# Another order of the first batch's loads, with a new job order and new PSUM banks, in a fused Linformer attention and MLP mixer

## The chip, the cores and the metric

The kernel runs on one core of one Trainium2 chip. The metric is the time of one execution in microseconds (us) on the device. The kernel before took 418.57 us, the median of 3 runs (417.91 to 418.78). One further execution was profiled. All instruction times below come from that one.

## The reference

```python
# q, k, v: (8 batches, 8 heads, 1024, 64); E, F: (64, 1024)
k_proj = einsum('ks,bhsd->bhkd', E, k)
v_proj = einsum('ks,bhsd->bhkd', F, v)
scores = scale * matmul(q, k_proj^T)              # 1024 x 64 for each head
attn = softmax(scores)
x = matmul(attn, v_proj)                          # -> (8, 1024, 512), heads side by side
h = maximum(x^T @ w_tok1, 0) @ w_tok2             # tokens: 1024 -> 256 -> 1024
u = x + h^T
h2 = maximum(u @ w_ch1, 0) @ w_ch2                # channels: 512 -> 1536 -> 512
out = u + h2                                      # (8, 1024, 512) float32
```

## The kernel before

The work is a pipeline over eight batches. The kernel does not emit its instructions as it goes through its loops. It first collects some 2,200 jobs in a `Planner` (each job is a few instructions of one engine, or one DMA) together with what each job reads and writes. `plan()` then returns the jobs in one sequence, and the last loop (L1521) emits them in that sequence, so each engine and each DMA queue gets its own jobs in the order in which they stand in it.

Nothing is decided by costs at that point. The sequence is written out by hand in three constants at the top of the file:

- `ORDER` (L15): the whole sequence, two characters for a job. The characters 0 to 9, A to Z, a to z, + and - stand for 0 to 63, so "0R" is job 27 and "7L" is job 7 x 64 + 21 = 469.
- `SPOTS` (L62): for each use of PSUM, which of the eight banks it takes. A job that takes a bank waits until the last reader of the bank's use before has finished.
- `FILLS` (L69): places in the sequence. Ahead of each a matmul on zeros is put in, `blank(zero)` (L436, 128x512, result unused). A place that is listed three times gets three.

For each batch the jobs are these.

- **Loads.** GpSimd (POOL in the profile) issues them with `dma` (L358), one for 2 or 4 heads of q, k or v. Batch 0 is loaded in pairs of heads, in pieces of 0.5 MB in the source, together with the token weights (`wt1` in two halves, `wt2`) and then the channel weights (`w1`, `w2`). A new load waits, where its buffer was in use, for the last reader.
- **Projection** of k and v with E and F (L521), copies to bf16 `kb`, `vb` (`copy`, L334 on DVE, L336 on ACT). E and F are themselves transposed first (L462, taken over at L465).
- **Transposes of k and q.** From batch 2 on these are DMA transposes, which SyncE (SP) issues: `k_transpose_dma` (L558, all heads at once) and `turn_q` (L600, four heads each, two for a batch). In batch 0 TensorE (PE) makes them: `k_transpose` (L574) and `q_transpose_pe` (L618).
- **Attention.** Scores (L637) from `qT` and `kT`, exp on ACT (L652), the product with `vb` (L672), the reciprocal of the sums (L686) and the scaling to `x_sb` (L692), both on DVE.
- **Token mixing.** In batch 0 it runs by pairs of heads as well: `token1_part` (L1060, ReLU L1075), `token2_part` (L1092), then `u_transpose_pe` (L1121). Later batches use a scheme of seven products instead of eight blocks (L875, L991) and transpose u by DMA (`turn_u`, L784, tile uT).
- **Channel mixing.** The same scheme of seven products: `up_set` (L1180, with ReLU L1202, copies L1208 and L1223, additions on DVE L1161 and L1216), `down_block` (L1289), the residual addition (L1336) and the store of the output (L1327, from POOL, in the last batch also from SP and ACT).

Two more things order the transfers. `load_group` and `q_transpose` tie transfers to one another ("loads and transposes take turns"): each of the two q transposes of a batch waits until the last q load of that batch has landed, and the next load of q waits for the transposes that read its buffer. And SP issues its transposes strictly one after another, in the sequence's order.

The opening goes, for each pair of heads: load k, v, q; project (PE); copy k (ACT or DVE); transpose k (PE); copy kT; transpose q (PE), copy qT (1.01 us on ACT); scores (PE); two exps (1.1 us on ACT); attention product (PE); x (DVE); token products (PE).

Of the kernel before, what the change touches and what calls it, by code (L numbers as in the profile page):

```python
# [12 lines left out]
ACT = mybir.ActivationFunctionType  # L13
EARLY = 12.0
ORDER = (  # L15
    "0R000T0Q090P0S0102040W050U0X030V0A1+061-2007240s080v0w0t0u250x0C0z0+0D0y0-111L0B101M1E0E181G1B151C19"
    "1F0H1A1J261I1K1H1D12271N13140G16171P1O0F1W1c1X1Y1T1g1Q1Z1f1e1R1d1S1j0I1U1V1h1k1a1i281b2N0J291l2S1n2O"
    "2T1m0K2P2Q2A1o1u2U1p2R1v1x1r1q3C211s1t2V1y222X232W2Y1w2E1z2H2B2K2F2I2Z2C2a2L2J2l3B2b2D2h2G332M2i2c0M"
    "2d2e342f2p2m2g0L352x2q362t2y2j0O2r2u2k2n372o0Y2-380N2s2v3L302w2z393M0c3D3v0Z2+313I3N3H323d0a3E3O3J3j"
    "3e0d4c0e3P3A3f3Q0f3h0g3g3R9w3F3i0b3S3K3w3-0h3k3T0i3x4Y3l3U3V3y3z3G3m3W3X4a4d5p3Y4Z3+4e3Z6B0j3p4f403q"  # L20
    "5r4g414u4h425A5s3n4v0k4j3o455B4y464k4w4b434z0l4i445E4l4x4m3a4-4n474o3r5q5C4p4B5D0o4+503t4C9v5F495251"
    "4D5H0p5u4J0q5v535w3b5I0m54485x5y555KA15t3c4G5z0n4H565L4q4K3u576D4A4I5+6F4L6E4M3s6C6H6G6O4N6A6P6Q6160"
    "6I9x6R62696L5-4E6J6S6T4O6f6Z6367646g6h4F686a6M6K654s4Q6bA2660r4R4r6N6c6U4P5S6V4S6W4U6d6e4T6Y6i6o6u6X"
    "6j6l6k5T6m6n6r6x6p5U4V6q6s6y6+6z5G6-4W5a705b4X6t5J74717A72736v5M756w77765N785O585Q7B79595c5X7C5R5Y7J"
    "7H7K7F7I7Q7D7G7S7EA55Z7L7R4t5d5PA6A75eA8AA5VA3A45f5W5h5g7M5i7N5lAD5j7O7V5k7Z7W7X7n7a7Y5m7PA97o7d5n7b"
    "7e7T7p7c7r9z7q7g7s7f7hAF7u7iAH7jAG9-7l7U7v7t7mAJ83AI7wAN7x84AOAhAK7zAi7yALAM877kAjAQ857+88Ak8986AP8A"
    "ARASAbAlAm8BAWAcAdAeAX8D8CATAZ8LAfAgENAaAU8F9y8EAEAVB38MAY8GEO8mB4B5AnAt8iAB8n8+AoAz8k8N8oAC7-8q8pAu"
    "5o8T8H8rAv8U818-8jAq8tA+Ap928JAw90A-93Ar8QAs918lB68uAxB095Ay8K9G96B7B18wB8B28s8xB98R9HBBBD988v9K8S99"
    "9IBEBC94EQBF9+EP8yBGBA8W97BI8zBH9A8V9L8X9BBJ9J9NBK9M829OBL8IBN8YBM9QBOA0BV9RBPBR8aBWBSBTBQBk80BYBl8b"
    "BZBaBXBUBcBb8OBd8P9PBfBnBeBp9SBgBhBmBiERBoBjBq8Z9YES9CET9Z9TEWBr9a8e9E8f9UBs9g8cBu9hBt8dC19WEZBzBwC2"  # L30
# [24 lines left out]
    "TRTMVGTSTlTmVRTnVTVSTQSsVUVWTTStVVVXTUSuTWTVVZVYTNVaToVbTXSkTYVdSwTpSxVcTuVeTvTqVfSlTwSyVgW1VlSzU0Vh"
    "SvVpW2U1VnVqViU2W3W5TrS+VjW6TsVtW4VkTaS-VuVmVrVoTzT0VwT1W8VxVvW9T+WBT-W7WCVyWJVzTZWKV-VsTtU3WAV+WLW0"
    "WNWzU4WOWDWMU5X0TbWbWETxWyWQW+WPWRU7X1WSTyWFU8X2U9WcU6UAWTWdWHX4WUWVW-X5UBWWUCWGXIWXWZWjWIX7UDXaX8Wg"
    "XJX6X3XMX9WkXNXAWlWhWaXbXKWiXCWYXeWmWnXcWoXPXDXOXQWqXfXRWrXLXhWsXgXiXUWtXjXSUEWeXVXTWfXdXEXFXkWpXmXl"
    "XWXsXBXnXtXoXYWuXuXGXqWvX-WwXxXXWxXyXpXHXzXrXZXvY9XwY0X+Y1Y4Y2Y3Y6Y5Y7YAYDY8YBYJYFYEYMYGYLYNYHYKYQYI"
    "YCYOYRYP"  # L60
)
SPOTS = (  # L62
    "1722467307234441203466116170466360762302312744331670103172245374067253415210734175262102125107667450"
    "1520620612306606413423170354767105253604361302764621303237243176464774171176417604252570156254404366"
    "2373521237102235700221317730106123406106503414727325704746701646213666333167646254435756374205316107"
    "3513126156167122221112015160746532017414020057236736457430642470552552655172151277014703436566371016"
    "1004135333425222002277525207405235256117403572635617204"
)
# [119 lines left out]
def kernel(  # L188
# [1376 lines left out]
```

## Time and profile before

| | |
|---|---|
| median of 3 runs | 418.57 us |
| the profiled execution, its own time | 419.06 us |
| its span, first to last instruction | 417.3 us |
| outside the span | 1.8 us |
| PE busy in the span | 407.7 us (98%) |
| DVE busy | 356.8 us (85%) |
| ACT busy | 221.6 us (53%) |
| end of the last matmul | 412.05 us |

The profile counts an engine as busy from an instruction's start to its modelled end, so matmuls that follow each other closely overlap. For small waits the distance from one matmul's start to the next is the finer measure: in a run of 256-column matmuls it is 109 ns, in one of 512 columns 216 ns. Rows of the timeline have the start, the duration, the engine, the line and operation, the tiles and the number of instructions, and in brackets the idle time ahead with what ended it. The profiled execution is 0.49 us longer than the median of the runs.

### The profile page before, as it was taken

To read this page: it belongs to the slowest core of one execution; us is meant where nothing else is said; L and a number is where in the kernel's file an instruction comes from. 1 tells how busy PE (TensorE), PEld (TensorE's weight loads), DVE (VectorE), ACT (ScalarE), POOL (GpSimd) and SP (SyncE) were. 2 spreads that over 40 slices of the span, in tenths; PEclk is the share of its full clock that TensorE was granted. 3 is DMA by queue.
4 is the path that set the end of the run, shared out by engine and by line. 5 is a ranking of instruction groups with operands and counts; after the bars stand their busy time and mean duration, and the time that the engine had idled before them with its cause. 6 is when DMAs were issued, how large, how long until landed. Compare 5 with 4: busy or idle time off the path is not lost.

```text
span 417.3 us, 9605 instructions
## 1 busy us (share of the span) xinstructions
PE 407.7 (98%) x3911; PEld 344.6 (83%) x3913; DVE 356.8 (85%) x773; ACT 221.6 (53%) x429; POOL 66.8 (16%) x105
## 2 busy tenths in 40 slices
PE   8999999998999999999999999999999999999995
PEld 4489888687888888989988889888889789988884
DVE  2479899778999999989989898889989899978685
ACT  1658884267536564483654555455644755344340
POOL 8453021012102030101201011023000001010010
PEclk9999999999999999999999999999999999999999
DMA  8999999597998997997958599898984402250134
GB/s 165 206 200 205 207 191 193 154 150 128 202 190 161 158 190 123 198 154 149 210 95 170 106 203 161 155 174 138 226 122 115 101 0 102 52 151 11 43 117 137
DMA packets 93900, 61.70 MB, mean 148 GB/s; under 512 B 59040, under 2 KB 89376, under 8 KB 93856
## 3 DMA queue, kind: packets, MB, share of 16 engines
q0 software_dynamic: 35088, 45.09, 56.0%
q1 hardware_dynamic: 58128, 15.27, 22.1%
q10 hardware_dynamic: 640, 0.72, 0.5%
q8 instruction: 30, 0.49, 0.4%
q14 instruction: 14, 0.11, 0.1%
HBM read 59.24 MB, written 16.78 MB: 182 GB/s over the span
## 4 chain that ended last, share of the span: by engine, by line
PE 82%; DVE 9%; DMA 5%; POOL 1%; issue 1%; SPq 1%; ACT 0%; DVEq 0%; POOLq 0%
PE psum L1289 31%; PE psum L1180 30%; PE psum L991 4%; PE psum L875 4%; PE psum L521 3%; DVE x_sb L692 3%; DMA qT<-q_sb 3%; PE psum L672 3%; DMA k_sb<-in_k_dram 2%; PE psum L637 2%; DVE G L1161 1%; DVE G L1216 1%; PE psum L1092 1%; DVE rdn L686 1%; PE psum L712 1%
## 5 line engine op out<-in xcount | busy, mean ns | idle before, releaser
L1289 PEld LDWEIGHTS <-G 128*128 128x128 bf16 x1356 | 130.0, 98 | 18.0 <-issue 3.1
L1289 PE MATMUL psum<-wc_sb,G 128*128 128x256 bf16 x780 | 101.0, 271 | 0.0
L1180 PEld LDWEIGHTS <-wc_sb 128*128 128x128 bf16 x768 | 73.9, 98 | 9.5 <-issue 1.4
L1289 PE MATMUL psum<-wT,G 128*128 128x256 bf16 x576 | 76.1, 273 | 0.0
L1202 ACT ACTIVATE G<-psum 128x512 bf16<-128x512 f32 x96 | 56.4, 601 | 28.4 <-PE psum L1180 27.8
L1216 DVE TENSOR_TENSOR G<-G 128x512 bf16<-128x512 bf16 (+1 forms) x140 | 68.8, 515 | 0.4
L1180 PEld LDWEIGHTS <-wT 128*128 128x128 bf16 x576 | 55.4, 98 | 8.5 <-issue 1.9
L1180 PE MATMUL psum<-S,wT 128*128 128x256 bf16 x384 | 56.7, 273 | 0.0
L1327 POOL DMA_DIRECT2D out_dram<-o x30 | 16.4, 547 | 250.5 <-DVE o L1336 183.8
L1180 PE MATMUL psum<-S,wc_sb 128*128 128x256 bf16 x384 | 56.3, 273 | 0.0
L1180 PE MATMUL psum<-uT,wc_sb 128*128 128x256 bf16 x384 | 56.1, 273 | 0.0
L692 DVE TENSOR_TENSOR x_sb<-psum,rdn 128x256 bf16<-128x256 f32 (+1 forms) x88 | 46.9, 542 | 2.1
L1336 DVE TENSOR_TENSOR o<-psum,u 128x512 f32<-128x512 f32 x59 | 40.3, 684 | 7.4 <-PE psum L1289 6.5
L1223 ACT COPY psum<-psum 128x512 f32<-128x512 f32 x48 | 27.7, 579 | 27.1 <-PE psum L1180 18.4
L1161 DVE CUSTOM_DVE_ANT_0 G<-psum,ua 128x512 bf16<-128x512 f32 x48 | 32.6, 683 | 7.4 <-ACT ua L1208 4.0
L652 ACT ACTIVATE a<-psum 128x512 bf16<-128x512 f32 x64 | 34.6, 605 | 8.2 <-PE psum L637 8.2
L1208 ACT COPY ub<-psum 128x512 f32<-128x512 f32 x48 | 28.3, 589 | 19.1 <-PE psum L1180 11.3
L1208 ACT COPY ua<-psum 128x512 f32<-128x512 f32 x48 | 28.2, 592 | 17.5 <-PE psum L1180 17.4
L1161 DVE CUSTOM_DVE_ANT_0 G<-psum,ub 128x512 bf16<-128x512 f32 x48 | 32.8, 684 | 2.8 <-PE psum L1180 2.5
L1180 PE MATMUL psum<-uT,wT 128*128 128x256 bf16 x192 | 28.8, 273 | 0.1
L672 PE MATMUL psum<-vb,a 128*128 128x130 bf16 x256 | 25.0, 220 | 0.2
L686 DVE RECIPROCAL rdn<-psum 128x4 f32<-128x4 f32 (+1 forms) x88 | 15.3, 184 | 9.9 <-PE psum L672 9.2
(102 smaller groups left out, 497.8 us busy)
## 6 DMA issues: line engine op xcount, KB each, us to landing
out_dram<-o POOLq DMA_DIRECT2D x30, 512.0 KB, 4.5
v_sb<-in_v_dram POOLq DMA_DIRECT2D x14, 512.0 KB, 8.0
k_sb<-in_k_dram POOLq DMA_DIRECT2D x14, 512.0 KB, 10.2
q_sb<-in_q_dram POOLq DMA_DIRECT2D x14, 512.0 KB, 9.3
wc_sb<-in_moe_w_ch_dram POOLq DMA_DIRECT2D x6, 256.0 KB, 11.4
wc_sb<-in_moe_w_ch_dram POOLq DMA_DIRECT2D x4, 384.0 KB, 14.3
k_sb<-in_k_dram POOLq DMA_DIRECT2D x4, 256.0 KB, 6.4
v_sb<-in_v_dram POOLq DMA_DIRECT2D x4, 256.0 KB, 8.5
```

What stands on the lines that cost most here:

```text
L652: lambda g=g, half=half, bk=bk: nc.scalar.activation(out=a_t[g][:, half], in_=bank(bk), func=ACT.Exp, scale=scale),
L672: nc.tensor.matmul(view()[:, k, c].rearrange("p i d -> p (i d)"), a_t[g][:, c, at : at + P], vb[:, g].rearrange("k i d -> k (i d)"), start ...
L686: lambda: nc.vector.reciprocal(out=rdn, in_=view()[:, :, :, :, D]),
L692: lambda: nc.vector.tensor_tensor(out=x_sb[:, rows, g * P : (g + 1) * P].rearrange("p (n c) (i d) -> p n c i d", c=2, i=2), in0=view()[:, ...
L1161: nc.vector._custom_dve(TENSOR_ADD_SAT, out=out, in0=in0, in1=in1, s0=FMAX, s1=0.0)
L1180: nc.tensor.matmul(t[:, c, :], w1_of(n, dd, 2 * m + c), a_of(j, n, dd), start=(n in (1, 7) and c == 0 and dd == 0), stop=(c == 1 and dd == 1),
L1202: lambda: nc.scalar.activation(out=G[:, n, cs], in_=view(src), func=ACT.Relu),
L1208: 512, lambda: nc.scalar.copy(out=dst, in_=view("y")), writes=[(name, s % 2)],
L1216: 512 * len(both), lambda: f(out=G[:, n, c], in0=G[:, a, c], in1=G[:, b, c]), ps=False,
L1223: 512, lambda: nc.scalar.copy(out=view("y"), in_=view("x")), takes=[bk["y"]],
L1289: nc.tensor.matmul(to, G[:, G_OF[n], cc, t * P : (t + 1) * P], w2_of(n, cc)[:, cut], start=(n in opens and (t == 0 or alone) and cc == 0), ...
L1336: 512, lambda: nc.vector.tensor_add(out=dst, in0=view(src), in1=u_of(sh, dh)),
```

## The change

Only the three constants differ. The jobs, what they read and write, and all instructions but the fills are the same.

```diff
 ORDER = (
-    "0R000T0Q090P0S0102040W050U0X030V0A1+061-2007240s080v0w0t0u250x0C0z0+0D0y0-111L0B101M1E0E181G1B151C19"
...
-    "7H7K7F7I7Q7D7G7S7EA55Z7L7R4t5d5PA6A75eA8AA5VA3A45f5W5h5g7M5i7N5lAD5j7O7V5k7Z7W7X7n7a7Y5m7PA97o7d5n7b"
...
+    "0R030T0Q050P0S0408060U070W0V001L0X011M02091E0A1F1G1I1H1J0B1K1N1j1O0C1P1k1c0D1Z1d1Q1e1g1f1h1i0E1R1S1l"
...
+    "6l6e5T6m6n6x6+6v5U6o4V6-6y6z716p5a6q4W5G705b725J746r7A73756s765M6t776wA35N7B5O585Q787C5R4t5X5P795Y7J"
+    "7F7K7D7G7H7Q7EA57I5Z7L7R5dA759A85eA65VA95fAAA45W5c5h5g5i7V7S5l7TAD7Z7X4X5m5j7a7n5k5n7b7o7W7d5o9z7M7e"
...
 )
 SPOTS = (
-    "1722467307234441203466116170466360762302312744331670103172245374067253415210734175262102125107667450"
...
+    "3024101126436327273643040127120236363170420436171063240217145624732113405063774765765024721257605205"
...
 )
-FILLS = (17, 17, 22, 22, 23, 30, 30, 30, 36, 36, 36, 36, 36, 42, 42, 53, 53, 70, 70, 70, 70, 70, 70)
+FILLS = (21, 21, 21, 21, 21, 21, 21, 27, 27, 30, 36, 36, 36, 36, 49, 62, 62, 66, 66, 79, 79)
```

Read as jobs, the sequence changes in these places.

**The loads of batch 0 on POOL** (k2 is k of heads 2 and 3; wt1a and wt1b are the halves of the first token weight; w1 and w2 are pieces of the channel weights; the identity matrices are made on POOL between the first load and the second in both):

```
place   1   2   3   4   5   6   7   8   9   10  11    12    13   14    15
before  k0  k6  v0  q0  v2  q2  k2  q6  k4  v4  q4    wt1a  wt1b v6    wt2  w1 ...
after   k2  q2  v2  q4  k4  v4  k0  v0  q0  k6  q6    v6    wt1a wt1b  wt2  w1 x6, w2 x2, k v (batch 1), w2 x2, q ...
```

**The pairs of heads on PE.** Before, k of pair 6 (heads 6 and 7) is projected first of all, then k and v of pairs 0, 2 and 4, and v of pair 6 last; q is transposed, and the scores follow, in the order 0, 2, 6, 4. After, k and v are projected for pairs 2, 4 and 0, then k and at last v of pair 6; q and the scores go 2, 4, 0, 6. The q transposes of pairs 2 and 4 now stand ahead of the projection of the same pair. The two halves of the first token weight land before v6 in the one and after it in the other.

**The fills** are 23 before and 21 after; seven of them now stand ahead of the first projection.

**SP's transposes around batch 2.** Job 643 ("A3") is the q transpose of batch 2's heads 0 to 3, job 644 that of heads 4 to 7, 650 ("AA") the k transpose of the same batch, 469 ("7L") a transpose of u, and 653 ("AD") a load of 4 heads of v for batch 3 on POOL, which waits for the k transpose.

```
before  469 uT    650 kT    643 qT    644 qT
after   643 qT    469 uT    650 kT    644 qT
```

The q transposes of later batches move ahead on SP in the same manner, and a store of the output moves behind the load 653. In batch 6 the loads v (1440), q (1681) and k (1438) stand in another order behind a store. In the last batch the last two PE jobs and the last stores on SP and ACT change places. Many single jobs of PE, DVE and ACT between these stand a few places earlier or later, and most uses of PSUM have another bank.

More of the change, by code (lines that the diff above doesn't have):

```diff
@@ L26 @@
[L26 to L30, printed above, removed]
@@ new lines @@
+    "1T1m1W1X0s1U0H0u0w0t0v1n0z0G0x0+1+0F0y0-201-101a1Y24111b1V26250J1812271B19151A1621130I14281C1D1u291o"
+    "172S230K2A2T221p1r1q2N2O1v1s2B1t2E1x2P0M2C2U1w2Q1y2V2F1z2R2X2K2W2D2Y2H2G2Z2a2L2I2c2J2b2d2M2l0L2x2m2h"
+    "2y2e3B2f2n2i2g2p2o2z3C2q2t2+2-2u2j2r0O302k332v2s0Y37342w310N3L0Z0a353M3d3I3H3D3v323J3N36383R3O0c3E3P"
+    "3e0d4c0e3Q3j3K0g3h0f393F3i0b3S3A3f3T3k0h3g3U3-3l3V3G0i3w3X9w3n3W3Y3z4d3m3x3+4u4Y3y4a3p4v4Z403q4g410k"
+    "4w3o5A424x4y0l5B4e0j4h5p4b4f454j464i4k3r5C4z0m43475D5E4l444-0o4m503s4o4n3t4+4p5q525t514B5F4q5r4C495s"
@@ new lines @@
+    "530p544D3Z5y3u5w0q5H3bA15x4J3c3a6B5u5I554K5z4r4G4L5K5v4A4H9v5L9x6D484I5+6E0r6F564M6C5-6G6O4N6A606P6Q"
+    "626H6I6L4O636561646Z6J674s666K4EA26a57684F6M6b696N4Q0n6f4P6U6g6R6W4R6S6h6Y4U4S6V6c6i6T6X5S4T6d6j6k6u"
+    "6l6e5T6m6n6x6+6v5U6o4V6-6y6z716p5a6q4W5G705b725J746r7A73756s765M6t776wA35N7B5O585Q787C5R4t5X5P795Y7J"
+    "7F7K7D7G7H7Q7EA57I5Z7L7R5dA759A85eA65VA95fAAA45W5c5h5g5i7V7S5l7TAD7Z7X4X5m5j7a7n5k5n7b7o7W7d5o9z7M7e"
+    "7p9-7c7O7q7g7P7r7h7N7f7sAF7i7uAH7Y7lAG7t7m7v7jAJ837wAIANAK7x84ALAOAhAM7z7yAiAP877kAj857U7+88AQAb8986"
@@ new lines @@
+    "ARAS8AAcAdAk8BAWAlAm8L9yAZ8CAYAeAT8DAfAaAg8FAUAXAV8M8G8EENB3At7-Az8N8mAEA+8+8i8n8TA-EO8k8oAuAvABAn8H"
+    "8U8pB4B5AC8-8q81B0Aq8r92Ao8J90Ap938QArAs8jB6AwB18tB2B795Ax8uB88R8l91Ay8s96B9948v8w9G978x8yBB9H988SBD"
+    "999I8KBE9KBCBF8z8WBGEP8VEQ9L9ABABI9N9BBJBH9O9+8X9JBKBNA0BLBO8Y9QBM829MBPBRBSBV8I8aBWBQBTBk9R80BYBXBl"
+    "8bBZBUBn9PBc8OBdBa9SBeBfBpBbBh8PBgBmBiER9CBj8ZBo9YEVES9TBr9ZEUBqET8eBs9aEW8f8c9UBu8d9g9W9E9hEYBtC1Bz"
+    "9dEZC2B-9iBwC59VC3BxC69eC48gC89D8hEbC9Bv9bEdC0Ec9c9FEfEj9fCBEeEgEkElCC9jB+EmEhEi9kEn9XEpEr9lC7EoCFCA"
@@ new lines @@
+    "By9nCGEsEtCDEq9oCEEu9mCJCHEvEwExCI9r9pCKCXEyEz9qCLCYCME+CNCZEaE-F09sCaILCOCPF19tIMCbDACREXCcF2F4F3Cd"
+    "CQ9uF5CeF6CpCfF7FBDCChCSFCDEF9CqDFFADSCiCgFDCrDICTFEDGDJF8FGCjFHFFDHFLDTFICxCkFMFJFPClDUCmFKDLDBDVFQ"
+    "FNDDDMFTCVCyINFUFRFODKCnFWDWFXCuDXDNFYCvCzFaCwFVDZFbDQDaC+DRFiFcDODcFSDPFZFdFfFeIPFjFgDdCUFhFlIRDYIT"
+    "DkDbISCsIQCWDlFkIUIOC-CoFmFnDeD0CtFoFpDoFqD2DpD1D3FxIXDmD4D6DnIWFzFsFrDrD5FtDqDsFuF-DtD7G0DfDuD8G1Dv"
+    "DwF+G2DgG3E0FvG4E1DiDxFwIZE2DyG6IbD+E8G7DjE9IcDzIdGDEAIaE5FyGEG9DhIeGAE6IfD-IhIgGHIiGFIjGIG5GGIkG8IY"
@@ new lines @@
+    "GVInE7GKMKIoGBImEBGCGLIsIlECItIuIpGNIqIrIvGOE3IwEDGWE4IxI-GZJ0EEIyGaEFJ1EGIzI+EJEHGXJ5EIJ2GYGcJ3J4GJ"
+    "MJGdHQJ7IVJ9J8GbJAD9H8GfGeJBHCGMJCGhJ6JEH9GPJFGiJDGgJJHAHDJGEKHRGQJHJKGRHGJIGTHEHHMLJLMMJNHSJMHUGSHT"
+    "HJHVJOGnJPELHFJRHKGjJTEMHXHBJSGlGoJUGpHIJVHMHLJWHNGsGUHYJYHiJQJZHaJXGtHbHOHjJbHPGvJaHmHWJcHnJgJdGwJe"
+    "MNGuJfGxGmHZGyMPGkJhHpHcMOJjMRHkMSMQJkGzHlHdHoHqHeJnGqHrJlJoHsGrMVG+HtHuG-JiJzJmH0J+HvH4JpH1JvJsH2H+"
+    "JtJqH3H-HwJxJ-I0JwH5JrK0K1JyJuHyMXK2HxI6MYHgMaK4HzH6I7MZK5HfKBI3I8KCK7MbHhMcK8KDMdQIMeMfKEKFMgMTMhI4"
@@ new lines @@
+    "KGK3I5MiK6KIMmI9KJIAMjMkKLIBMnKMK9MoMpKTMlKHKAKUMqI1MrMsQKIDL7MtKXMuMvKZKYIEKKMwL6KVIFKaL8I2IGMxKbMy"
+    "KNKWH7ICKdMzKcKeLgM+LAM-IHLBKON0IIN1N3LEN2KfLFKlKgLON5KmLPIJN7KhIKLCN6N8LHMWN4N9LILSL9QHNAKPLQLDNCMU"
+    "KiLRNBNDLKLTNENHKRKnLGKjNFLJLVNGKSKqNILLNJLhLMNKLWKrLNNPNLKtNMNQNNKkLiNOKsNSLkNTLYKuKQLZNWLjQJNUNXKw"
+    "LlNVKoKvKpNZNRKxNYLUNaNeNbLnNcQLLXNfNdKyKzLaQMNhQOLbNjLmLoNiK+QNLpQPNgQQK-LcLqL0NlLrL2LeL1LsNmLyLtQT"
+    "LzLuNnNoL+L3NtLwNxNkM4NyL4NqO9LxL5M5NvOANwNzNuOBM6N+M1NpOCODNrN-OEM2O0NsQVM3O2QWLvO1LdO3M7QXO4O5QYOG"
@@ new lines @@
+    "O7OHM8O8QZOFO6M9QaL-OIQdLfOJOLQeQbOKQfMBOMM0QcMCMAQgMDQlQkMFQmMEQnQhORQjP4QUMGP6QiONQRP8OSQoP7P9OXQS"
+    "QpQqOVUGPAMHOWQuUFOTPBQvQwOYOUMIQrPCOZQsQtOjPDOaQxQ+PFQyQzObQ-OdR0OcPMOePGOkPNP5PIR1R5PJR3PEOlOPPOPQ"
+    "OfPPOrOhR6PHPROsR4R7R2PTR8PSPURAR9RBOoRCPVOpOgUIRFOQRDRGOqPWREPKOtPXPeRJRHOiPfRKRNRLPYRIROOuPLRQPZUH"
+    "PiRRPgRcOOPhRSOvRMRTRPRUOwUJRdRVPjRWPaRXUNRfUKRZRYOyULRaRhUMPlRgRbReUOPmPwRiPkRjPnPxRkOzPcPoOmO+PpRl"
+    "RmPyO-PqRnOnRrRoQ2RtOxRvPrQ3RwRpP0Q4RqP1RxP2S7RyPsRzPuUPPbR+P-UQRuPvURS0RsQ0S8S1UUSBUVQ1S9SCS3UWSAQ5"
@@ new lines @@
+    "PdUTUXS4SEUYUZUSR-SDSFS2UaSGQ6UbUdS5Q7SJUePtUfUcQ9UgUhSPT3SHSKSQUoQASIUpS6STT2UrUqSUSRT6UsSSQBSWUlUt"
+    "QCSXPzUmT7T4P+UnUiQ8TASZUjUkShSLT8UxUuT9QDUvSaUwSVUzQESYU-SiU+V0TBSbT5QFV1TCSNV2QGTDSjUyV4P3TETcScV5"
+    "V3TFSpV6SqSdSOV9SfV7VASeTGTdVDSMTKV8THTeSrTIVHTJVBVISmVETLVFVCSnVKTgVLVMThTMSoVJTfVOVGTjTNVPVWTkTOVQ"
+    "TiTPVRTlVTSsVNStVUVXTRVSTmTSSgVZVVTQTnVaTuTTToSuSkTpTWTqSwTXSxTYVdVYSySlTsSzTvVeTUSvVbVlTVVgVpVnS+Vf"
+    "VqVcS-TwVmVtT0U0VuVoT1W1VhU1W2TaViVwVjVrVxU2W5VkWJW6VvWKTzVyT+WNT-V-W8W0VzU3WOW9W7VsU4WAV+WQTrWPTZWR"
@@ L61 @@
+    "WLWSW3WDU5W4X0TtWBWyWTTbWCXIWMWzWVW+WUTxWEX1TyWFU7U6U8WWX4W-U9UBWXWbUAWZX2XaX3UCX5WcXbUDXJX7WYXcWdWH"
+    "X6XdWGXMX8WgXNX9WhXPXCXQXAXDXeWiWjXfWaXOXBXEXKXGWmXRXLWIWkXUWlWnXVXhWoWeXiXWXgWqXjWrXmWfXnXkXoXSWsXs"
+    "XTWpWtXtXlXHUEXYWuXZXuXpWvXqXFX-XXX+WwXxWxXyXvY9XzXrY0XwY1Y4Y2Y3Y6Y5Y7YAYDY8YBYJYFYEYMYGYKYNYHYLYOYI"
+    "YCYQYPYR"
 )
 SPOTS = (
-    "1722467307234441203466116170466360762302312744331670103172245374067253415210734175262102125107667450"
-    "1520620612306606413423170354767105253604361302764621303237243176464774171176417604252570156254404366"
@@ L68 @@
+    "1713476526117451111000431363504562017414020567306256407306640427552552201753173152014723475602015723"
+    "0720475332734202200176315612415716323744645200150524671"
 )
[L69 removed]
+FILLS = (21, 21, 21, 21, 21, 21, 21, 27, 27, 30, 36, 36, 36, 36, 49, 62, 62, 66, 66, 79, 79)
 WHOLE = 3
```

43 lines of the change are left out of this document (2 added, 41 removed).

## The prediction

> **What bounds the kernel now.** I read the busy times first, then the forty slices, then each engine's busy time by stretches, then the waits around the slices where PE is not full.
>
> ```profile
> PE 407.7 (98%) x3911; PEld 344.6 (83%) x3913; DVE 356.8 (85%) x773; ACT 221.6 (53%) x429; POOL 66.8 (16%) x105
> ...
> PE   8999999998999999999999999999999999999995
> ...
> DMA  8999999597998997997958599898984402250134
> ```
>
> PE is the bound. Its slices are full but for the first, the tenth and the last. So the change, which leaves every instruction but two fills as it is, can only win or lose where PE waits. The stretches tell how much there is (columns: start and end in us, length, busy time of PE, PEld, DVE, ACT, POOL, granted clock, DMA share, GB/s):
>
> ```profile
> 0.00:10.40 10.40, 8.70 (x45) 4.39 (x45) 2.13 (x8) 1.87 (x2) 8.69 (x19) 1.00 0.88 165
> 10.40:20.90 10.50, 9.53 (x105) 5.14 (x103) 4.59 (x17) 6.40 (x16) 5.19 (x8) 1.00 1.22 206
> 20.90:31.30 10.40, 10.05 (x153) 8.82 (x152) 8.03 (x29) 5.30 (x12) 5.73 (x8) 1.00 1.33 200
> 30.00:98.00 68.00, 66.76 (x667) 55.26 (x667) 59.57 (x149) 44.95 (x86) 11.59 (x17) 1.00 1.10 185
> 98.20:412.00 313.80, 313.57 (x2971) 272.07 (x2971) 282.97 (x574) 164.02 (x316) 36.32 (x56) 1.00 0.70 136
> ```
>
> Length less PE's busy time is 1.70, 0.97 and 0.35 us in the opening, 1.24 us from 30 to 98 and 0.23 us in all the rest. The fourth is one wait:
>
> ```profile
> PEld L637 <- DMA qT<-q_sb: 1.4, 1, 1.4
> PE psum L637 <- DMA qT<-q_sb: 1.2, 1, 1.2
> ```
>
> The scores of batch 2 stand still until the second q transpose of SP has landed. SP's own rows show its issues, and the DMA view from 85.6 to 93.1 the times from issue to landing of the two transfers that met:
>
> ```profile
> 79.54 1.92 SPq L784 DMA_TRANSPOSE uT<-u  x1
> 82.17 1.21 SPq L558 DMA_TRANSPOSE kT<-kb  x1
> 83.56 9.43 SPq L600 DMA_TRANSPOSE qT<-q_sb  x2
> ```
> ```profile
> v_sb<-in_v_dram POOLq DMA_DIRECT2D x1, 512.0 KB, 10.3
> qT<-q_sb SPq DMA_TRANSPOSE x1, 12.4
> ```
>
> Two q transposes were issued at 83.56 and 85.64; the v load 653 was issued on POOL at 85.20, because it waited for the k transpose ahead of them. The second transpose took 12.4 us to land, the load 10.3. The load of the same size between 55 and 65, with no transpose beside it, took 6.5.
>
> Smaller waits don't show as idle time. From the distances between successive matmul starts I count those of over 60 ns after 35 us: besides the one at 98 they come to about 4 us, nearly all of 0.06 to 0.24 us each.
>
> **Step 1, the wait at 98.** The new order has SP issue the transpose of heads 0 to 3 first. It waits for nothing but batch 2's second q load, so it goes out at about 71.3. The uT keeps its time (79.6), the kT follows at about 82.2, and the second q transpose at about 83.4, one issue earlier than now. The v load comes behind the kT as now (about 84.7, packets from about 86.5), when this transpose has had 3 us. A transpose without a load beside it landed in about 4.4 us, so I put it at 88 against a use at 96.7. The wait goes: **−1.23 us** (−1.39 by matmul starts). Next late there is nothing over 0.1 us: the other inputs of that stretch are PE's and DVE's own.
>
> **Step 2, the opening.** POOL's landings form a grid of one pair of heads in about 1.28 us. Before, they were at 5.81, 7.18, 9.81, 11.05, 12.33, 13.62, 14.93, 16.17, 17.46, 18.74, 20.74, 21.43, 22.68, 23.99 and 26.45 (wt2). The third is some 1.35 us late and the eleventh 0.7. I take both as belonging to the place and not to the tile, as nothing shows otherwise. I then walk through the new order: an instruction starts when its engine is free and 0.05 us after its last input, and lasts as its row says. The same walk over the old order has the first channel product (L1180) at 33.09; the trace has 33.46. Durations are those of rows such as these:
>
> ```profile
> 20.78 0.62 PE L618 MATMUL psum<-ident,q_sb 128*128 128x128 bf16 x8 [0.19 <-DMA q_sb<-in_q_dram]
> 21.76 0.41 PE L637 MATMUL psum<-qT,kT 64*64 64x512 bf16 x4 [0.29 <-DVE x_sb L692]
> ...
> 21.44 1.01 ACT L336 COPY qT<-psum 128x1024 bf16<-128x1024 bf16 x1 [0.25 <-PE psum L618]
> 22.35 2.19 ACT L652 ACTIVATE a<-psum 128x512 bf16<-128x512 f32 x4
> ```
>
> New order: v2 lands 9.81, its projection starts 9.86, scores of pair 2 at 11.83; v4 13.62, projection 13.67, scores 15.70; k, v, q of pair 0 at 14.93, 16.17, 17.46, projection 16.36, q turned 17.51, copied 18.64 to 19.65, scores 19.88; k6 18.74, projected 18.79; q6 20.74, turned 20.80, copied 21.82 to 22.83, scores 22.88, two exps until 24.67. From 24.85 PE has the attention and token products of all pairs and is nearly gapless. Idle up to 41 us comes to 4.96 us on the old order and 5.71 on the new: +0.75. Two fills fewer take 2 x 0.216 = 0.43 off the path where they stood ahead of work that was ready. Together **+0.3 us**. With every hand-off 0.05 us slower it is up to +1.2; a whole grid 1.3 us later is +1.3. Where the two late places don't come back, the opening gains up to 1.4 instead.
>
> **Step 3, the small waits.** The walk over the rest finds 3.3 us of waits on the old order after 41 us and 2.5 on the new (other PSUM banks, jobs a few places apart). It misses a fourth of the waits that the trace has, so I take half of its gain: **−0.4**, bounds +0.2 and −0.85.
>
> **Step 4, transfers that meet elsewhere.** The transpose of 71.3 meets a k load that would land at 73.9 and is needed at 78.6: hidden by 4.7 us unless it is slowed like 653. In batch 6 the k load 1438 lands at about 260.8, needed at 263.9, beside a transpose from 258.3 on. The uT transposes have 0.6 to 1.6 us to spare. Other loads that overlapped a transpose in the trace were 0 to 1.1 us slower. I take **+0.1**, bounds 0 and +1.2.
>
> The two last matmul jobs that change places, and the last stores, leave the tail of 5.2 us behind the last matmul (412.05) as it is: 0.
>
> **Sum.** −1.23 + 0.3 − 0.4 + 0.1 = −1.23. The profiled execution took 419.06 us (span 417.3 and 1.8 around it) and would take 417.8. It stood 0.49 above the median of 418.57, so the forecast is **417.3**. What a measurement of this kernel can tell from no change I put at 0.2%, 0.84 us: faster is below 417.7, slower above 419.4.
>
> **A rule that speaks against step 4's price.** The row is the 12.4 us of the transpose beside the load's 10.3. The Trainium skill, page "DMA: Bandwidth & Descriptors", section "Queues, rings and completion order", says that each DMA engine serves the queues that have work in turn, a packet at a time. Shared evenly like that, 4.4 us of transpose and 2.6 of load packets would both be over in about 7 us, an estimate by that page's rule; the trace does not agree, at 12.4. By the rule step 4 would be 0 and the sum −1.33.
>
> **Rivals.**
>
> *A. The wait moves (0.23).* The early transpose slows the k load at 71.3 as 653 was slowed (10.3 against 6.5, and later): landing 79.8 for a use at 78.6, +1.2 on PE; or the same in batch 6. For it: the only meeting of a q transpose with a load issued within 2 us cost the most. Against it: 4.7 us of cover, and the milder overlaps. Time: 417.3 + 1.0 = 418.3, within 0.2%.
>
> *B. The last pair comes late (0.22), the slower side.* Place: pair 6, now last in everything: k6 and q6 at places 10 and 11, then projection, copies, transposes, the 1.01 us copy of qT, scores, two exps, attention. Before, q6 was there at place 8 and only v6 came late. That chain ends about 0.5 us ahead of PE's need at 24.85; each us of delay beyond that is one of PE. It decides when q6 lands after about 23.3 (20.74 + 0.5 + 1.23 won elsewhere + 0.84). Two more late places of 1.35 ahead of q6, less 0.5, plus the 0.4 by which the walk fell short on the old order (ACT has the qT copies and exps of three pairs back to back) make 2.6: 417.3 + 2.6 = 419.9. For it: single places were 1.35 and 0.7 late before. Against it: both are in the walk already.
>
> *C. The opening gains too (0.10).* The late places don't come back: 417.3 − 1.4 = 415.9.
>
> *D. The clock (0.02).* The longest PE gap in the opening is 0.48 us now and about 0.6 in the new order, and two fills go. The rows show a slow state: 128x512 fills on bf16 zeros started 427 ns apart until 3.85 us and 216 ns apart later, while the granted clock reads 1.00 throughout. Half speed for 3.4 us would add 1.7: 419.0. The Trainium skill, page "TensorE: Matmul & The Clock Gate", section "What's actually happening", has this as half the clock by default and again after an idle window of about 3.4 us; the trace agrees with the first half (427 against 216), and none of its gaps is long enough to show the second.
>
> That the order doesn't become what its digits say I leave at nothing: the instruction lists of both kernels, engine by engine, show the moves told above.
>
> **Chances and range.** Forecast 0.43, A 0.23, B 0.22, C 0.10, D 0.02. Faster is forecast and C, 0.53; same is A and D, 0.25; slower is B, 0.22. The range goes from just below C, 415.7, to B's centre, 419.9, which leaves out half of B and a part of C.
>
> **What would show it.** Step 1: the scores of batch 2 start at 96 to 97 without a wait on qT, and SP's rows have a q transpose at 71. Step 2: the first L1180 product within 0.5 us of 33.5; B would show idle time ahead of L637 or L672 between 20 and 30, with ACT or a load as the releaser. Step 3: fewer distances of 60 ns and more between matmul starts. Step 4: a wait on a k, v or uT transfer after 70. Wrong would be the whole if PE's idle time after the opening grew although SP issued as told, or if a transfer's time changed by its place in a way that the old trace doesn't hold.

## The result and the profile after

The kernel after takes **417.30 us** (median of 8 runs, 416.87 to 417.54) against 418.19 us for the kernel before (8 runs, 417.41 to 418.78). The ratio is 0.9978, its 95% interval 0.9967 to 0.9988. On another chip it was 0.9971 (0.9961 to 0.9981). The forecast was 417.3 us and 1.23 us less; measured is 0.89 us less here and 1.26 us there. The kernel before, timed against itself as if it were a changed one, came to 0.9992 (0.9983 to 1.0001), so a ratio within 0.1% of 1 tells nothing.

The profiled execution after took 417.44 us, its span 415.7. Its page, the lines for PE as they were shown of before:

```profile
PE 406.6 (98%) x3911; PEld 344.3 (83%) x3911; DVE 355.8 (86%) x773; ACT 221.7 (53%) x429; POOL 66.7 (16%) x105
...
PE   8899999999999999999999999999999999999994
...
DMA  9999999896998797986947959783997212260124
```

The eight in the tenth slice, where the scores of batch 2 waited, has gone. There is one more in the second. The stretches (columns as before: start and end, length, busy time of PE, PEld, DVE, ACT, POOL, granted clock, DMA share, GB/s):

```profile
0.00:10.40 10.40, 8.78 (x45) 4.69 (x45) 2.25 (x7) 1.87 (x2) 9.11 (x19) 1.00 0.91 166
10.40:20.90 10.50, 9.16 (x107) 4.80 (x103) 3.70 (x15) 7.34 (x18) 5.50 (x8) 1.00 1.22 204
20.90:31.30 10.40, 9.93 (x160) 9.16 (x159) 9.12 (x31) 4.78 (x11) 5.25 (x7) 1.00 1.31 201
30.00:98.00 68.00, 67.94 (x678) 55.60 (x676) 59.84 (x149) 45.23 (x87) 11.92 (x18) 1.00 1.14 198
98.20:410.00 311.80, 311.41 (x2949) 270.91 (x2946) 281.03 (x571) 163.11 (x314) 35.76 (x55) 1.00 0.69 134
```

From 30 to 98 us PE now idles 0.06 us (1.24 before). In the opening it idles 1.62, 1.34 and 0.47 us (1.70, 0.97 and 0.35 before). SP's rows around batch 2:

```profile
70.71 5.51 SPq L600 DMA_TRANSPOSE qT<-q_sb  x1
79.17 1.70 SPq L784 DMA_TRANSPOSE uT<-u  x1
81.81 1.19 SPq L558 DMA_TRANSPOSE kT<-kb  x1
83.06 1.99 SPq L600 DMA_TRANSPOSE qT<-q_sb  x1
93.09 3.59 SPq L784 DMA_TRANSPOSE uT<-u  x1
```

The first q transpose goes at 70.71, the second at 83.06. The DMA view from 79 to 90 has the times from issue to landing of the second one and of the v load behind it:

```profile
v_sb<-in_v_dram POOLq DMA_DIRECT2D x1, 512.0 KB, 8.2
qT<-q_sb SPq DMA_TRANSPOSE x1, 4.3
```

It landed at 87.4 and was used at 96.4. One wait is new in this execution, near 318 us (engine, line, what it waited for: total, times, longest):

```profile
DVE S L807 <- DMA uT<-u: 1.1, 1, 1.1
...
PE psum L1289 <- DVE o L1346: 0.3, 1, 0.3
```

**An account of PE's waits.** Idle time in the profile misses small waits, so I use a finer account for all kernels: the time at which a job of PE starts, less the work of all jobs ahead of it (0.109 us for a matmul of 256 columns, 0.216 for 512, fills included, and so on). How much it grows over a stretch is what PE lost there, in us. The account cannot see which wait it was; the rows tell that. The columns are cut at fixed times, and the kernels reach the same job at different times, so a small wait near a cut falls into one column here and into the next there. The stretch from 40 to 97 us, for example, reads 1.39 to 1.48 in kernels whose PE jobs stand in the order of before there, and 1.39 to 1.61 in those with the order of after. Differences of 0.2 us in one column say nothing.

| profile | to 40 us | and fills | 40 to 97 | 97 to 105 | 105 to the end |
|---|---|---|---|---|---|
| before | 6.96 | 4.96 | 1.39 | 1.61 | 5.33 |
| before, second profile | 6.60 | 4.96 | 1.39 | 1.36 | 5.36 |
| after | 7.00 | 4.53 | 1.61 | 0.14 | 5.14 |
| after, second profile | 7.49 | 4.53 | 1.49 | 0.29 | 4.43 |
| e1 opening of after, rest of before | 7.42 | 4.53 | 2.06 | 2.05 | 5.37 |
| e2 before, q transpose first | 7.15 | 4.96 | 1.48 | 0.39 | 5.36 |
| e3 after, q transpose back | 7.36 | 4.53 | 1.40 | 4.51 | 4.49 |
| e4 after to 133 us, then before | 7.38 | 4.53 | 1.49 | 0.25 | 5.37 |
| e5 before, load waits | 6.93 | 4.96 | 1.48 | 4.03 | 6.52 |
| e6 e2 to 134 us, then after | 6.61 | 4.96 | 1.48 | 0.37 | 4.95 |
| e7 after, no fills | 13.58 | 0 | 1.39 | 0.24 | 5.47 |
| e10 after, first seven fills | 10.58 | 1.51 | 1.48 | 0.25 | 4.81 |
| e11 after, two fills less | 7.10 | 4.09 | 1.60 | 0.15 | 4.48 |
| e12 e11 with the end of before | 7.13 | 4.09 | 1.61 | 0.14 | 4.93 |

From the two profiles each: the opening with its fills 11.74 before and 11.78 after (0), 40 to 97 +0.16, which the cut alone can make, 97 to 105 −1.27, 105 to the end −0.56. Behind the start of the last matmul the span lasted 5.23 and 5.20 us before, 5.45 and 5.45 after: +0.23. The sum is −1.40, and the spans say the same: 417.3 and 416.7 against 415.7 and 415.5.

### The profile page after: what moved, and what is told of

Its sections match the earlier page's. It is cut to its first block, busy times and chain, and to the rows that moved or that the text cites. A ratio compares the mean times of both kernels' runs of the same rounds, so it can differ in the third digit from the quotient of the medians.

```text
span 415.7 us, 9593 instructions
## 1 busy us (share of the span) xinstructions
PE 406.6 (98%) x3911; PEld 344.3 (83%) x3911; DVE 355.8 (86%) x773; ACT 221.7 (53%) x429; POOL 66.7 (16%) x105
## 4 chain that ended last, share of the span: by engine, by line
PE 90%; DMA 4%; DVE 2%; POOL 2%; issue 1%; ACT 0%; POOLq 0%; DVEq 0%; ACTq 0%
PE psum L1289 35%; PE psum L1180 34%; PE psum L875 4%; PE psum L991 4%; PE psum L672 3%; PE psum L521 3%; DMA k_sb<-in_k_dram 2%; PE psum L637 2%; DMA uT<-u 2%; PE psum L736 1%; PE psum L712 1%; PE psum L1060 1%; DVE u L1105 1%; POOL k_sb L358 1%; POOL v_sb L358 1%
## 5 line engine op out<-in xcount | busy, mean ns | idle before, releaser
L1289 PE MATMUL psum<-wc_sb,G 128*128 128x256 bf16 (+1 forms) x780 | 101.5, 271 | 0.0
L692 DVE TENSOR_TENSOR x_sb<-psum,rdn 128x256 bf16<-128x256 f32 (+1 forms) x88 | 46.7, 540 | 1.8
L358 POOL DMA_DIRECT2D v_sb<-in_v_dram x18 | 13.4, 745 | 76.2 <-PE psum L1180 25.9
## 6 DMA issues: line engine op xcount, KB each, us to landing
wc_sb<-in_moe_w_ch_dram POOLq DMA_DIRECT2D x6, 256.0 KB, 11.5
```

What stands on the lines that cost most here:

```text
L358: return lambda: nc.gpsimd.dma_start(out=dst, in_=src)
L692: lambda: nc.vector.tensor_tensor(out=x_sb[:, rows, g * P : (g + 1) * P].rearrange("p (n c) (i d) -> p n c i d", c=2, i=2), in0=view()[:, ...
L1289: nc.tensor.matmul(to, G[:, G_OF[n], cc, t * P : (t + 1) * P], w2_of(n, cc)[:, cut], start=(n in opens and (t == 0 or alone) and cc == 0), ...
```

## The experiments

The theory at the start (A): the place of one q transpose on SP brings most of the gain, the opening little. The rival (B): the new order of the first loads brings it.

**e1, the opening of after, the rest of before.**

```diff
 ORDER, SPOTS
-jobs at places 0 to 329 as in before
+jobs at places 0 to 329 as in after, with after's fills
 the jobs that are left in the order and the banks of before
```

> The first 330 jobs (to about 57 us) in the order and the banks of after, the rest of before. Theory A (the q transpose that goes first on SP brings most of the gain, the opening 0.4 us of it): 0.3 to 0.5 us faster than before, ratio 0.9988 to 0.9993, and the wait of the scores on the second q transpose at about 98 us is still there with over 1 us. Theory B (the new order of the first loads brings the gain, and the wait at 98 was only one execution's): 0.9 us or more faster, ratio 0.9978 or less.

Measured: 420.31 us, ratio 1.0049 (1.0035 to 1.0062), slower by 1.8 us. Neither number came. The table tells why: the opening with its fills is 11.95, as in before; the wait at 99 us is there and longer (2.05), since the second q transpose took 12.8 us; and a wait of 0.7 us arose at 60 us:

```profile
PE psum L1289 <- DVE wait L1336: 0.5, 1, 0.5
```

There the rest of before meets a DVE queue that stands about 1 us later than its own opening would leave it. B falls: with the new loads and the old rest nothing is gained. The size says more: an opening and a rest that were not laid out for each other cost more than either differs.

**e2, the one transpose moved, in before.**

```diff
 SP's jobs of batch 2 in ORDER
-469 uT, 650 kT, 643 qT, 644 qT
+643 qT, 469 uT, 650 kT, 644 qT
```

> The kernel before with one job moved: the q transpose of heads 0 to 3 of batch 2 goes ahead of the u and k transposes on SP; all other engines keep their instructions. Theory A: the wait at 98 us is gone and the time falls by 1.0 to 1.4 us, ratio 0.9967 to 0.9976; the transpose is issued at about 74 us and lands by 82. Theory B: within 0.3 us of before. Third case: the early transpose meets a load and only moves the wait, within 0.3 us too, but with a wait on a k, v or u transfer between 74 and 98.

Measured: 418.14 us, ratio 0.9989 (0.9981 to 0.9998).

```profile
74.54 3.28 SPq L600 DMA_TRANSPOSE qT<-q_sb  x1
79.67 1.70 SPq L784 DMA_TRANSPOSE uT<-u  x1
82.36 1.19 SPq L558 DMA_TRANSPOSE kT<-kb  x1
83.65 1.94 SPq L600 DMA_TRANSPOSE qT<-q_sb  x1
```

The mechanism is as forecast: the transpose at 83.65 took 4.3 us where in before the one at 85.64 took 12.4, and 97 to 105 falls to 0.39. Compared job by job (by the start of the same PE instruction in both traces, each from the start of its span), PE stands 0.19 us behind before at 96 us, 1.06 ahead of it at 100 and 0.95 ahead at 105, and it stays there (0.91 at the end): the wait went and no other took its place. The time shows less. It fell by 0.4 us where 1.0 to 1.4 were expected, and the ratio cannot be told from that of the kernel timed against itself (0.9992). The opening differs by more than that between executions of one order (with its fills 11.57 to 12.11 in e6 and e2), so one profile of each cannot say where the rest of the gain is. That stays open.

**e3, the same transpose put back, in after.**

```diff
 SP's jobs of batch 2 in ORDER
-643 qT, 469 uT, 650 kT, 644 qT
+469 uT, 650 kT, 643 qT, 644 qT
```

> The kernel after with that one transpose put back behind the u and k transposes. Theory A: the wait at about 96 us comes back, 1.0 to 1.4 us slower than after, so 0.1 to 0.5 us slower than before, ratio 1.0000 to 1.0012. Theory B: as after, ratio 0.9978.

Measured: 420.71 us, ratio 1.0053 (1.0032 to 1.0073), some 3 us slower than after.

```profile
PE psum L637 <- DMA qT<-q_sb: 2.7, 1, 2.7
```

The wait comes back at more than twice its size. The reason is in the queue behind it: this order issues three stores of 0.5 MB right behind the v load (85.90, 87.07 and 87.81), that of before only one, and the transpose took 13.9 us while 2.1 MB of load and store packets went beside it, against 1.05 MB in before.

The wait is not the whole loss. These stretches are cut where the record of the granted clock (the eighth number) changes:

```profile
95.92:99.33 3.41, 0.93 (x10) 0.69 (x7) 2.51 (x8) 1.03 (x2) 0.00 (x0) 1.00 1.17 301
99.33:102.75 3.42, 3.16 (x21) 1.86 (x22) 0.41 (x2) 2.04 (x4) 0.00 (x0) 0.50 0.51 115
```

Behind the wait TensorE ran at half its clock for 3.4 us. Job by job against the second profile of after, e3 is 0.1 us ahead at 96 us, 2.7 us late at the first scores behind the wait and 4.15 us late at 102.7: the wait cost 2.8 us and the clock another 1.5. The other runs fit this for the most part: 420.61 and 420.81 us with the profiled one's mean clock of 0.993, 419.24 and 419.41 at 0.997; the slowest, 422.26 at 0.996, does not. In the order of after the early transpose is worth 3 us; in that of before some 0.4. What one edit is worth depends on what the rest puts beside it, and on whether the wait becomes long enough for the clock to fall.

**e4, after to 133 us, then before.**

```diff
 ORDER, SPOTS
 jobs at places 0 to 776 as in after
-the jobs that are left as in after
+the jobs that are left as in before
```

> After up to its 777th job (133 us), before from there on; both orders have done the same jobs at that point. The profile of after shows a new wait at 318.6 us (a u transpose that took 6.3 us, 0.7 us of TensorE in all), which the order of before does not have there. Theory A with that wait as a loss of the later part: 0.5 to 0.8 us faster than after, ratio to before 0.9959 to 0.9968. If the wait at 318.6 is one execution's and the later parts are worth the same: as after, 0.9978. If the later part of after is the better one in the mean: 0.9985 or more.

Measured: 417.89 us, ratio 0.9986 (0.9978 to 0.9995): the third case. The later part of after is the better one in the mean, although its first profile had the wait at 318; the intervals of e4 and after overlap a little, the profiles do not. From 105 us on, the kernels that end in before's order lost 5.33 to 5.37 us in five profiles (e5 aside, of which below), those with after's later part 4.43 to 5.14 in seven (e7 aside, which lost 0.8 us near 354).

**e5, the load kept away from the transpose.**

```diff
+    load, turned = pl.jobs[653], pl.jobs[644]
+    load.deps.add(turned)
+    tied[load] = turned
     plan = pl.plan()
```

> The kernel before with one wait changed: the v load of batch 3 (653) waits for the second q transpose of batch 2 (644), not for the k transpose, so that load and transpose no longer overlap; SP's order is that of before. Theory A (the load beside it makes the transpose slow): the transpose, issued at 85.6 us, lands after 4.3 to 5.5 us, by 91, and the scores at about 97 no longer wait. The load then lands at about 97.5 and the u transpose behind it at about 102, against a use at 99.8, so a wait of about 2 us on uT takes its place and the time is 0.3 us faster to 1 us slower than before, ratio 0.9993 to 1.0024. Rival (two q transposes one behind the other on SP make the second slow, load or no load): it still takes over 10 us, the scores still wait, and the u transpose comes later on top, 3 us or more slower, ratio 1.007 or more.

Measured: 422.72 us, ratio 1.0102 (1.0088 to 1.0116).

```profile
83.53 4.71 SPq L600 DMA_TRANSPOSE qT<-q_sb  x2
98.89 2.19 SPq L784 DMA_TRANSPOSE uT<-u  x1
```

```profile
PE psum L1180 <- DMA uT<-u: 3.2, 1, 3.2
```

Two answers. The second q transpose, issued at 85.60 directly behind the first as in before, landed at 92.1 after 6.5 us, and the scores don't wait: it was not the transpose ahead of it that made it slow, but the load, together with the store that POOL issues right behind the load and that moved with it (86.43 in before, 93.42 here). Which of the two does how much, this run cannot say. (It was not the 4.3 us of a transpose alone; one 16 KB packet of the instruction queue fell into it at 90.1.) But the load now lands at 98.8 and the u transpose, which waits for it, goes at 98.89 instead of 95.56 and lands at 103.2: a wait of 3.2 us takes the place of the other. The time is that of the rival, its cause is not. I had the transpose land by 91 and the load at 97.5; they landed 1.1 and 1.3 us later, all of it on the path of the u transpose. Then the clock fell, as in e3:

```profile
100.56:103.97 3.41, 0.70 (x9) 0.66 (x10) 0.76 (x2) 0.01 (x1) 0.00 (x0) 1.00 0.69 125
103.97:107.39 3.42, 3.42 (x21) 2.49 (x19) 3.29 (x11) 2.06 (x4) 2.67 (x4) 0.50 0.24 38
```

Job by job e5 is 2.1 us behind before when the wait ends and 3.7 at 107.6: the half clock cost 1.6 us. The one of its five runs with a mean clock of 1.000 took 421.34 us, the others 422.69 to 422.89.

**What goes on while they overlap.** The DMA view counts the packets of each queue; q0 carries POOL's loads and stores, q1 SP's transposes:

| profile, stretch (us) | packets on q0 | MB on q0 | packets on q1 | MB on q1 |
|---|---|---|---|---|
| before, 90 to 94 | 409 | 0.63 | 402 | 0.10 |
| e3, 92.5 to 97 | 508 | 1.55 | 505 | 0.13 |

The two queues advance packet for packet, although a packet of the transpose has 256 bytes and one of the load 1 KB (4 KB in a store). The transpose needs some 2,000 packets. It got about 100 in a microsecond here, and some 850 with nothing beside it (e5, 86 us). So the queue with the small packets is the one that is held up.

**e6, the later part alone.** Before with the one transpose moved, and from place 774 on as after.

```diff
 ORDER, SPOTS
 jobs at places 0 to 773 as in e2
-the jobs that are left as in before
+the jobs that are left as in after
```

> Before with the one q transpose moved ahead, up to its 774th job (134 us), and from there the order and banks of after; both orders have done the same jobs at that point. It is after with the opening of before. Theory: the later part of after has 0.85 us fewer small waits where no u transpose comes late, and the opening is worth 0.2 us: 0.3 to 0.8 us faster than the kernel with the one transpose moved, ratio to before 0.9970 to 0.9982, within 0.3 us of after. Rival (the opening brings the rest of the gain): as the kernel with the one transpose moved, 0.9987 to 0.9992.

Measured: 417.70 us, ratio 0.9981 (0.9970 to 0.9992), in the range of the theory. Together with e4 this says that the later part is worth some 0.4 us (e2 0.9989 to e6 0.9981, e4 0.9986 to after 0.9971 or 0.9978), and that the new opening adds at most 0.1%. The intervals of e2 and e6 overlap, so by the times alone this is a likely reading; the profiles have it too: job by job e6 gains 0.41 us on e2 from 134 us to the end, although its u transpose at 312 came late.

**e7, no fills.**

```diff
-FILLS = (21, 21, 21, 21, 21, 21, 21, 27, 27, 30, 36, 36, 36, 36, 49, 62, 62, 66, 66, 79, 79)
+FILLS = ()
```

> After without its 21 fills; the four matmuls on zeros at the very start stay. Theory A (fills stand in TensorE's waits for loads and cost and bring nothing): within 0.4 us of after. Theory C (they stand ahead of work that is ready): up to 21 x 0.216 = 4.5 us less at most, of which some 0.5 to 1 us would show. Rival (they keep the clock): after the wait of about 1.5 to 2 us ahead of the first projection the matmuls of 128 columns start 107 to 110 ns apart instead of 57 for some microseconds, and the time is 1 to 3 us longer than after.

Measured: 419.24 us, ratio 1.0018 (1.0007 to 1.0029), 2.0 us slower than after on the same chip. Two stretches of this kernel, cut again where the record of the clock changes, and below them two of other kernels, e1 around its wait at 99 us and e10 (below) in its opening, after which the clock stayed at 1.00:

```profile
6.87:10.28 3.41, 1.21 (x12) 0.82 (x11) 1.38 (x2) 0.37 (x1) 2.74 (x4) 1.00 1.17 161
10.28:20.52 10.24, 8.69 (x89) 5.91 (x89) 2.07 (x9) 5.39 (x15) 5.48 (x8) 0.50 1.21 200
```

```profile
97.44:100.85 3.41, 1.75 (x23) 1.13 (x21) 2.40 (x10) 1.75 (x4) 0.00 (x0) 1.00 1.08 232
8.41:11.83 3.42, 1.97 (x22) 0.88 (x20) 1.28 (x5) 0.27 (x1) 1.94 (x4) 1.00 1.12 169
```

The granted clock is 0.50 for 10.24 us, three times 3.41. The four products of scores at 12.68 are busy 0.64 us, at full clock 0.41. PE was never without work for more than 1.5 us; it was busy 1.21 of the 3.41 us ahead of the fall, 35%. The Trainium skill, page "TensorE: Matmul & The Clock Gate", section "What's actually happening", has half the clock after at least one idle window of about 3.4 us; the half agrees with the 0.50 here, and so does the length, but a window with 35% work in it was enough. In the fourteen profiles, cut into such steps, the clock fell behind every step in which PE was busy 37% or less (27% in e3, 21% in e5) and behind none with 50% or more (51% in e1, 58% in e10). Between the two there is no case.

The opening lost 1.6 us against the second profile of after, job by job. Another 0.8 us is a wait of PE near 354 us, which no run ties to the fills.

**e8, after once more.** No edit.

> The kernel after, unchanged, for another look at its profile and a time on the same chip as the others. If the wait at 318.6 us was one execution's, the u transpose there takes 4.2 to 4.5 us and TensorE waits under 0.3 us between 316 and 322; if it belongs to the order, it takes about 6.3 us again. Ratio to before 0.9970 to 0.9985 either way.

Measured: 417.22 us, ratio 0.9971 (0.9961 to 0.9981). The u transpose at 312.81 took 4.2 us and PE did not wait. In all kernels that have the later part of after, it took 4.2 or 4.3 us in five profiles (e3, e7, e8, e10, e11) and 5.9, 6.3 and 6.0 in three (e6, after, e12). The order does not decide it: with the later part of before it took 4.3 us in four profiles and 5.8 and 6.2 in two (e4, e5). What does is open. Its cover is 0.8 to 0.9 us, so it costs nothing in the one case and 0.4 to 0.7 us in the other. In before the cover is 3.6 us.

**e9, before once more.** No edit.

> The kernel before, unchanged, for a second look at its profile. The ratio is 1 within 0.1%. Theory A with a wait that differs between executions: the second q transpose of batch 2 again takes over 9 us beside the v load, and TensorE waits for it at about 98 us for 0.4 to 2 us. If the wait is gone (under 0.2 us), it was the first profile's own, and the gain of after has to come from elsewhere.

Measured: 418.31 us, ratio 0.9992 (0.9983 to 1.0001). The wait is there again:

```profile
PE psum L637 <- DMA qT<-q_sb: 1.0, 1, 1.0
```

The transpose took 12.2 us beside the load.

**e10, only the first seven fills.**

```diff
-FILLS = (21, 21, 21, 21, 21, 21, 21, 27, 27, 30, 36, 36, 36, 36, 49, 62, 62, 66, 66, 79, 79)
+FILLS = (21, 21, 21, 21, 21, 21, 21)
```

> After with only the seven fills ahead of the first projection; the 14 later ones are left out. If the clock needs the later ones too: the granted clock falls below 1.00 between 12 and 24 us and the time is 1 to 2 us longer than after, ratio to before 0.9995 to 1.002. If the first seven are enough: the clock stays at 1.00 and the time is within 0.4 us of after, or up to 0.4 us shorter, ratio 0.9960 to 0.9980.

Measured: 418.14 us, ratio 0.9988 (0.9977 to 0.9999), with a wider spread than any other kernel, 416.58 to 418.98. Both cases came, by execution: the mean clock of the whole run was 0.999 at 416.58 us, 0.998 in the profiled one (417.68, granted clock 1.00 in every stretch of the opening), 0.995 at 417.42 to 418.14, 0.991 at 418.01 to 418.82, and 0.987 and 0.985 at 418.74 and 418.98. So with seven fills PE stands near the edge at which the clock falls; its profiled execution has five steps of 3.41 us in the opening with PE busy 58 to 74%. That an execution decides it fits the same section of the Trainium skill, which calls the window free-running.

**e11, the last two fills left out.**

```diff
-FILLS = (21, 21, 21, 21, 21, 21, 21, 27, 27, 30, 36, 36, 36, 36, 49, 62, 62, 66, 66, 79, 79)
+FILLS = (21, 21, 21, 21, 21, 21, 21, 27, 27, 30, 36, 36, 36, 36, 49, 62, 62, 66, 66)
```

> After without its last two fills, which stand ahead of the turning of the last pair's q. In one profile of after that q landed at 19.71 us and its turning started at 20.33, behind both fills; in another it landed at 20.45, when the fills were done. If fills lie on the path: 0.1 to 0.43 us faster than after, ratio to before 0.9961 to 0.9972, and the q is turned within 0.1 us of its landing. If they lie in a wait: within 0.1 us of after. If the clock hangs on them: it falls below 1.00 and the time is 0.5 us or more longer.

Measured: 417.08 us, ratio 0.9969 (0.9958 to 0.9979). The opening with its fills falls from 11.5 and 12.0 to 11.2. The last pair's q landed at 19.57 and was turned at 20.09, and not within 0.1 us: the row names a scaling on DVE (L692) as the releaser, not the load. So 0.24 us of 0.43 were left to win against after (20.33), and the timing can't tell the kernel from after (0.9971 to 0.9978). One of its 8 runs had a mean clock of 0.993 and was the slowest (417.94).

**e12, e11 with the end of before.**

```diff
 ORDER, SPOTS
 jobs at places 0 to 2177 as in after
-the jobs that are left as in after
+the jobs that are left as in before
```

> After without its last two fills, and from its 2178th job (406 us) in the order and banks of before, which differ there only in which of two last pieces of the output is computed and stored first. In the kernels that end in the order of before the span ended 5.15 to 5.23 us after the start of the last matmul, in those that end as after 5.30 to 5.47. If the order of the last pieces makes this: 5.15 to 5.25 us here, and a time 0.1 to 0.2 us below that of the kernel without the last two fills, ratio to before 0.9962 to 0.9972 (more than the timing can tell from it). If it is chance: 5.3 us or more.

Measured: 416.84 us, ratio 0.9970 (0.9961 to 0.9979). The span ends 4.93 us after the start of the last matmul, below the forecast of 5.15 to 5.25. With the six other kernels that end as before (5.15 to 5.23) against the seven that end as after (5.30 to 5.47), this says that the order of the last pieces makes the 0.2 us or somewhat more. e11 and e12 are the fastest kernels here; that they beat after is not shown by their intervals.

## Why the prediction was right, step by step

**Step 1, the wait at 98 us (−1.23): right**, in size (−1.27 from two profiles each) and in mechanism. e5 shows that the load and the store behind it made the transpose slow, and e2 that an issue 2 us earlier is enough. In the time of e2 alone the gain does not show in full, as said there.

**Step 2, the opening (+0.3): too dear by 0.3.** It came to 0 (11.74 to 11.78, fills included). The walk's starts were up to 0.7 us late against the trace: scores of pairs 2, 4, 0 and 6 at 11.75, 15.38, 19.49 and 22.16 us for 11.83, 15.70, 19.88 and 22.88. The part that failed is "belonging to the place", by half. The third load landed at 8.67 to 9.86 us in the five profiles of the old order and at 8.74 to 10.30 in the nine of the new; by the fourth load all fourteen stand 0.8 to 1.7 us behind a grid of 1.28 from the first. This lateness belongs to the start of the queue, and its size to the execution. The eleventh load was 0 to 0.7 us late on the tenth in the old order and 0 to 1.2 in the new: that is the execution's alone. As the walk took a late grid for granted on both orders, most of the error cancels in the difference.

**Step 3, the small waits (−0.4): right sign, half the size.** The walk gave −0.85 and I halved it, because it missed a fourth of the waits. Job by job from 134 us to the end, the second profile of after gains 0.87 us on before; the first gains 0.15, with the late u transpose of step 4 in it. A walk that misses some waits on both orders was the better guide undiluted. The waits that went are those of 0.15 to 0.24 us at 155, 247, 301, 335 and 344 us in before; e4 and e6 show that they belong to the later part's order and banks.

**Step 4, transfers that meet elsewhere (+0.1): right.** The early transpose took 7.5 us beside the k load, which landed at 73.8 for a use at 78.3, and the transpose at 78.2 for a use at 90.3: both hidden, so rival A did not come. The u transpose with little cover does cost, in three of eight profiles, 0.2 us in the mean (0.4 to 0.7 three times, 0 five times).

**The tail (0): wrong by +0.23 us**, the only term I had no row for. e12 shows it to be the order of the last two pieces.

**The sum** was −1.23, by the profiles −1.40, by the times −0.89 and −1.26. Between the profiles, the opening is 0.3 us better than its term and steps 3 and 4 together 0.26 (−0.56 for −0.3); the tail (+0.23) and 40 to 97 us (+0.16, which the cut can make) go against them. Errors of 0.2 to 0.3 us on both sides nearly cancel. That is luck in part.

**The rivals.** B, the last pair late, did not come; q of pair 6 landed at 19.6 to 21.0 us in the nine profiles with the new loads, never near 23.3. C did not come either. D, the clock, did not come with 21 fills, but e7 and e10 show that its chance hangs on the fills, which I had costed only by the time that they take. Its price of 1.7 us for one step of 3.4 us at half speed was nearly right: 1.5 in e3 and 1.6 in e5. That e7 is 2.0 us slower is no test of it: there the clock was low for three steps, and 4.5 us of fills had gone. What I did not see at all is that a wait like that of step 1 can bring the clock down too, once it is 2.7 us long.

**Even sharing of the DMA engines.** The Trainium skill, page "DMA: Bandwidth & Descriptors", section "Queues, rings and completion order", has each DMA engine serve its queues in turn, a packet at a time. From this the prediction estimated that both transfers would end in about 7 us; together they took 10.3 and 12.4, while e5 has the load at 6.1 us with only the store beside it and the transpose at 6.5 without either. The prediction took this as the trace speaking against the rule. The packet counts above are what turns of one packet each would give; it is the estimate that fails. It took turns for equal shares of the bytes, and left out the store.

## What to carry to other kernels

Look for the transfer that is late, then for what runs beside it: moving one transpose ahead in its queue, past work that does not need to come first, took a wait off the bound engine, while moving the load instead only moved the wait. Price such an edit in the order in which it will stand, since the same move was worth 0.4 us in one order and 3 us in another. Before removing idle-time matmuls, ask what the clock does without them, and ask the same of a long wait: 2.7 us of waiting cost another 1.5 at half clock (e3). And compare two traces job by job: an account cut at fixed times moves small waits from one column into the next.

## What the runs showed of the hardware

- The granted clock fell to 0.50 for 10.24 us when PE had been busy 35% of 3.41 us, with no gap above 1.5 us (e7), and for 3.41 us behind waits of 2.7 and 3.2 us (e3 with 27% busy, e5 with 21%). It did not fall behind 51% (e1) or 58% (e10). With seven fills it fell in some executions of the same kernel and not in others (e10).
- A transpose beside loads and stores advances packet for packet with them: 402 packets of 256 bytes against 409 of 0.63 MB in 4 us (before), 505 against 508 of 1.55 MB in 4.5 us (e3).
- A transpose of four heads of q took 4.3 us with under 0.04 MB beside it, 6.5 with one 16 KB packet of the instruction queue in it (e5), 7.5 with 0.81 MB of load and store packets beside it (after), 10.1 with 1.46 MB (before, the one at 112 us), 12.2 to 12.8 with 1.05 MB (before, e9, e1) and 13.9 with 2.1 MB (e3). The bytes alone do not set it.
- The same u transpose, at 312 to 318 us, took either 4.2 to 4.3 us or 5.8 to 6.3, by execution.
